# A routed two-layer kernel: a raw weight ring of ten, scaled results inside the next short visit, a relu moved from VectorE to ScalarE

## The chip, the cores and the metric

One core of one Trainium2 chip runs the whole program in one launch. The metric is the time of one execution on the device in microseconds (us). Names used below: TensorE (PE in the rows; PEld is its weight load), VectorE (DVE), ScalarE (ACT), GpSimd (POOL), and SyncE (SP), which issues most of the transfers.

## The reference, cut to what matters

```python
# q, k, v: (8, 8, 576, 64): banded attention (window 128), heads side by side give x: (8, 576, 512)
for b in range(B):
    prev_e = -1
    for s in range(S):
        fresh_e = int(np.argmax(logits[b, s]))
        e = fresh_e if s == 0 or local_gate[b, s] < 0.5 else (prev_e if prev_e >= 0 else fresh_e)
        prev_e = e
        p = softmax(logits[b, s])
        h = np.maximum(x[b, s] @ w1[e], 0.0)      # 512 -> 1024
        out[b, s] = p[e] * (h @ w2[e])            # 1024 -> 512
```

Each of the 4608 tokens goes through one of 8 experts. An expert is two matrix products with a relu between them, and the token's result is scaled with its probability.

## The kernel before, in words

The first third of the span computes attention and the routing. Then follow the **visits**: the plan (PLAN) holds 15 of them, three with the first tokens of experts 0 to 2 (256, 384 and 384 tokens) and twelve ordered by how full an expert is: 512, 272, 384, 232, 384, 232, 384, 200, 416, 264, 168 and 160 tokens. The change and the prediction deal with the last three, called here visit 264, visit 168 and visit 160.

**One visit.** It runs over 8 blocks f of 128 hidden units. For each block TensorE computes the first layer into a PSUM tile `h` (tiles `ah`, `al` of a weight chunk against the tokens' `qx`), then the second layer of the block before it into `y`: `second(f - 1)` stands behind the first layer of block f, and `second(7)` at the end. Every value is held as a coarse part and a remainder (hh and hl, `cut[:, 0]` and `cut[:, 1]`), so each product is three matmuls (lines L1331 to L1333). Between the layers ScalarE and VectorE turn `h` into `hh` = relu(h) and `hl` = relu(h) - hh.

**Visits under 200 tokens** (`both`, visits 168 and 160) compute the first layer in 8 wider matmuls per block (L1403, L1405) into two halves of `h`. ScalarE copies one half to `ha` (L1412), VectorE adds the other (L1413), VectorE makes `hh` (L1421) and `hl` (L1424).

**The partial window.** Tokens beyond a whole number of 128 (16, 8, 40 and 32 tokens in visits 272, 264, 168 and 160, likewise 32 in visit 416) take another way: ScalarE makes `hr` = relu (L1419), and `beside` multiplies it with the raw weight chunk (L1375) in `groups` row groups of one PSUM bank, 4 groups or, in visit 168, 2. At a visit's end `finish` scales the groups: ScalarE scales the first (L1340), VectorE adds the others one after the other (L1343). Whole windows are scaled by ScalarE (L1340) or VectorE (L1338). The scaled tile `y` is stored by an indirect transfer of POOL (L1318).

**Weights.** A weight matrix comes in chunks of 128 x 2 x 512 numbers (512 KB). `Stream.load` issues the transfer of chunk n into `wraw` (6 buffers) as soon as n is under the oldest chunk still needed + 6; a chunk that `beside` will read stays until it is read. `Stream.fill` cuts up to 6 chunks ahead: per chunk two casts by ScalarE (L310) and two subtractions by VectorE (L312) into `cut`. The buffer of a cut chunk comes free when the last matmul that reads it has run.

**Order.** In the visits the order of each engine's instructions is decided when the program is built, by a scheduler that keeps dependencies and places the rest by its own costs; on the chip each engine takes its instructions in that order. What it made of the change is shown below from the built programs.

Of the kernel before, what the change touches and what calls it, by code (L numbers as in the profile page):

```python
# [1 line left out]

# [1 line left out]

# [14 lines left out]
P = 128  # L19
# [15 lines left out]
RAWS = 6  # L35
SPLITS = 6
AHEAD = 4
EARLY = [(2, 5), (3, 6), (3, 6)]

def _plan():  # L40
# [55 lines left out]
def moe_attention(ctx, tc, qT, kT_d, vv, wg, wl, w1, w2, out):  # L96
# [199 lines left out]
            r.gate(t)  # L296
            r.turn(t)

    def load_chunk(e, which, c):
        src = w1 if which == "a" else w2  # L300
        t = wr.tile([P, 2, DM], F32, name="wraw")
# [13 lines left out]
    class Stream:  # L315
# [5 lines left out]
            self.raw, self.cut, self.gone, self.n_raw, self.n_cut, self.first, self.depth = [], {}, set(), 0, 0, 0, 1  # L321

        def load(self, ahead=RAWS):
            while self.n_raw < len(self.order) and self.n_raw < min([self.n_cut, *self.kept]) + ahead:
                e, which, c = self.order[self.n_raw]
                self.raw.append(load_chunk(e() if callable(e) else e, which, c))
                self.n_raw += 1

        def fill(self):
            while self.n_cut < len(self.order) and self.n_cut < self.first + self.depth:  # L330
# [995 lines left out]
    pending = []  # L1326
# [8 lines left out]
    def finish(o, m, g, col, alt, groups=1):  # L1335
# [8 lines left out]
        pending.append((col[:m], y[:m]))  # L1344


    class Fixed:
# [6 lines left out]
        def columns(self):  # L1354
            return 96 * self.rows.tokens + (24 * self.whole + 8 * self.part) * DM

        def run(self, W, tick):
            N = self.rows.tokens
            wins = [slice(P * t, min(P * t + P, N)) for t in range(self.n)]
            ys = [py.tile([P, DM], F32, name="y") for _ in wins]  # L1360
# [4 lines left out]
            both = N < 200  # L1365
            w = P * self.whole if m else N

            def beside(f):
# [12 lines left out]
                raws.clear()  # L1381

            def second(f):
                hh, hl = hs.pop(f)
                vh, vl = W.at("b")
                if m:
                    beside(f)
                for t in range(self.whole):
                    sl = wins[t]
                    three(ys[t][:sl.stop - sl.start], hh[:, sl], hl[:, sl], vh[:, f % 2], vl[:, f % 2], f == 0, f == 7)  # L1390
                    if t == (self.n + 1) // 2 - 1:
                        tick()
                if f % 2:
                    W.done("b")

            for f in range(8):
                ah, al = W.at("a")
                hp = ph_.tile([P, 2 * N if both else N], F32, name="h")
                for kc in range(4):
                    cs = slice(P * kc, P * kc + P)  # L1400
                    if both:
                        passed[0] += 3 * N
                        nc.tensor.matmul(hp.rearrange("p (two n) -> p two n", n=N), ah[:, f % 2, cs], self.rows.x[:, :, kc, :N],  # L1403
                                         start=kc == 0, stop=False, skip_group_check=True)
                        nc.tensor.matmul(hp[:, :N], al[:, f % 2, cs], xh[:, kc], start=False, stop=kc == 3, skip_group_check=True)  # L1405
                    else:
                        three(hp, ah[:, f % 2, cs], al[:, f % 2, cs], xh[:, kc], xl[:, kc], kc == 0, kc == 3)
                    if kc == 1:
                        tick()
                if both:  # L1410
                    ha = mp.tile([P, N], F32, name="ha", bufs=2)
                    now.act.copy(ha, hp[:, N:])  # L1412
                    nc.vector.tensor_tensor(ha, hp[:, :N], ha, ALU.add)  # L1413
                    hp = ha
                hh = mp.tile([P, N], F32R, name="hh", bufs=3)[:, :w]
                hl = mp.tile([P, N], F32R, name="hl", bufs=3)[:, :w]
                if m:
                    rest.append(mp.tile([P, 64], F32, name="hr", bufs=8)[:, :N - w])
                    now.act.activation(rest[-1], hp[:, w:], AF.Relu)  # L1419
                if both:  # L1420
                    nc.vector.tensor_scalar(hh, hp[:, :w], 0.0, None, ALU.max)  # L1421
                else:
                    now.act.activation(hh, hp[:, :w], AF.Relu)  # L1423
                nc.vector.scalar_tensor_tensor(hl, hp[:, :w], 0.0, hh, ALU.max, ALU.subtract)  # L1424
                hs[f] = (hh, hl)
                if f % 2:
# [5 lines left out]
            second(7)  # L1432
            for i, t in enumerate([self.n - 1, *range(self.n - 1)] if m else range(self.n)):
                c = self.rows.t0 + t
                finish(ys[t], wins[t].stop - wins[t].start, self.rows.g[:, t:t + 1], self.rows.idx[2][:, c:c + 1], i % 2 and groups < 4,
                       groups if m and t == self.n - 1 else 1)


    class Flex:
# [25 lines left out]
        def run(self, W, tick):  # L1465
# [49 lines left out]
            second(1, 0)  # L1515
            second(1, 1)
            finish(y, P, self.g, self.scol, 0)

    visits, tile_at = [], TO[0]
    for kind, e, at, nb, n in PLAN:  # L1520
# [93 lines left out]
    for i, v in enumerate(visits):  # L1614
        if isinstance(v, Fixed):
            upto = i + 1
            while upto < len(visits) and isinstance(visits[upto], Flex):
                upto += 1
            v.run(W, lambda: feed.tick(upto))
            feed.finish(upto)  # L1620
        else:
            v.run(W, lambda: feed.tick(upto, False))
# [56 lines left out]
```

## Time and profile before

| what | us |
|---|---|
| time of the runs, median of 3 | 669.78 (669.09 to 672.09) |
| time of the profiled execution | 671.84 |
| its span, first to last instruction | 670.1 |
| TensorE busy | 644.6 |
| VectorE busy | 512.4 |
| ScalarE busy | 412.9 |
| POOL busy | 370.6 |
| mean granted TensorE clock, share of full speed | 0.985 |

The span is what the profile's rows divide; the profiled execution took 1.74 us more than its span. A row of the timeline gives start and duration in us, engine, line, operation, the tiles written and read, the shapes, how many instructions were joined in the row, and in square brackets the engine's idle time before it and what ended it. "Busy" of TensorE is drawn from modelled ends, so two matmul rows may overlap.

### The profile page before, as it was taken

What the parts mean: (1) busy time and instruction counts of PE and PEld (TensorE: products, weight loads), DVE (VectorE), ACT (ScalarE), POOL (GpSimd) and SP (SyncE); (2) the same over time, 40 slices, a digit from 0 to 9 for tenths busy, and PEclk for the clock granted to TensorE, in tenths of its full rate; (3) what the DMA queues carried; (4) which work ended last, traced back from release to release, by engine and by line L of the source; (5) the groups of instructions that cost most, each with busy time, mean ns of one, the idle gap of its engine ahead of it and who ended that gap; (6) DMA issues with size and microseconds to landing.
All of it is one profiled execution on the core that took longest, in us unless ns stands there. A gap on an engine that the chain in (4) does not pass through costs nothing. (4 is left out here: it accounts for less than half of the span.)

```text
span 670.1 us, 17317 instructions
## 1 busy us (share of the span) xinstructions
PE 644.6 (96%) x5913; PEld 515.0 (77%) x5913; DVE 512.4 (76%) x1882; ACT 412.9 (62%) x1148; POOL 370.6 (55%) x567
## 2 busy tenths in 40 slices
PE   6999999999998989999999999999999999999995
PEld 3676766766665877899888889889988988888663
DVE  7899999999998799896454995675676576566883
ACT  4999999999887563344343554553555455455651
POOL 6456466455856776277651847557476466526411
PEclk7999999999998999999999999999999999999998
DMA  9863965853933674465632576666566574447640
GB/s 284 290 212 120 266 188 150 265 168 114 303 110 108 200 237 159 137 209 159 192 92 95 181 258 181 206 207 203 162 216 207 160 237 118 148 134 226 216 158 21
DMA packets 61964, 122.22 MB, mean 182 GB/s; under 512 B 9687, under 2 KB 28759, under 8 KB 61874
## 3 DMA queue, kind: packets, MB, share of 16 engines
q1 hardware_dynamic: 52322, 101.27, 47.9%
q0 software_dynamic: 9120, 19.24, 9.5%
q8 instruction: 47, 0.77, 0.5%
q10 hardware_dynamic: 432, 0.59, 0.3%
q14 instruction: 43, 0.35, 0.2%
HBM read 102.08 MB, written 19.04 MB: 181 GB/s over the span
## 5 line engine op out<-in xcount | busy, mean ns | idle before, releaser
L242 POOL DMA_INDIRECT kr<-xd,xidx x141 | 158.1, 1122 | 57.8 <-issue 41.6
L312 DVE TENSOR_TENSOR cut<-wraw,cut 128x512 fp32r<-128x512 f32 x232 | 151.4, 687 | 31.1 <-ACT cut L310 30.0
L310 ACT CAST cut<-wraw 128x512 fp32r<-128x512 f32 x222 | 127.0, 618 | 42.1 <-PE y L1333 40.2
L1331 PE MATMUL h<-qx,cut 128*128 128x384 f32 (+7 forms) x408 | 130.4, 320 | 1.7 <-ACT qx L253 1.7
L1332 PE MATMUL h<-qx,cut 128*128 128x384 f32 (+7 forms) x408 | 130.2, 319 | 0.1
L1333 PE MATMUL h<-qx,cut 128*128 128x384 f32 (+7 forms) x408 | 130.2, 319 | 0.0
L226 ACT ACTIVATE cut<-scs,mn 128x192 f32<-128x192 f32 (+2 forms) x288 | 121.1, 436 | 14.4 <-DVE mn L226 13.6
L1331 PE MATMUL y<-cut,hh 128*128 128x512 f32 (+2 forms) x288 | 115.4, 401 | 2.7 <-DVE hh L1421 2.7
L226 POOL TENSOR_SCALAR cut<-cut,r 128x192 f32<-128x192 f32 (+2 forms) x205 | 84.7, 429 | 58.6 <-DVE r L226 17.1
L1318 POOL DMA_INDIRECT out<-y,sidx x41 | 43.9, 1072 | 132.2 <-ACT y L1340 69.6
L1333 PE MATMUL y<-cut,hl 128*128 128x512 f32 (+2 forms) x288 | 114.2, 396 | 0.1
L1332 PE MATMUL y<-cut,hh 128*128 128x512 f32 (+2 forms) x288 | 113.6, 394 | 0.0
L1424 DVE SCALAR_TENSOR_TENSOR hl<-h,hh 128x384 fp32r<-128x384 f32 (+4 forms) x104 | 51.2, 495 | 64.2 <-ACT hh L1423 63.9
L1423 ACT ACTIVATE hh<-h 128x384 fp32r<-128x384 f32 (+4 forms) x98 | 43.7, 446 | 84.5 <-PE h L1333 81.2
L226 PE MATMUL sc<-kr,qx 64*64 64x192 f32 (+2 forms) x1152 | 83.0, 332 | 6.3 <-DVE mn L226 6.3
L1331 PEld LDWEIGHTS h<-qx,cut 128*128 128x128 f32 x408 | 77.4, 190 | 7.4 <-ACT qx L253 2.2
L1332 PEld LDWEIGHTS h<-qx,cut 128*128 128x128 f32 x408 | 77.7, 190 | 5.0 <-DVE qx L255 0.4
L1333 PEld LDWEIGHTS h<-qx,cut 128*128 128x128 f32 x408 | 77.7, 190 | 1.3
L226 PE MATMUL xa<-pts,cut 64*64 64x64 f32 (+1 forms) x1280 | 72.1, 254 | 2.5 <-ACT xT L226 2.2
L1331 PEld LDWEIGHTS y<-cut,hh 128*128 128x128 f32 (+2 forms) x288 | 53.5, 186 | 21.1 <-DVE hl L1424 3.3
L226 PEld LDWEIGHTS xa<-pts,cut 64*64 64x64 f32 (+1 forms) x1280 | 48.1, 135 | 23.9 <-issue 8.7
L226 PE MATMUL pt<-ident,cut 128*128 128x128 f32 x384 | 64.1, 289 | 0.7 <-POOL cut L226 0.7
(237 smaller groups left out, 1043.0 us busy)
## 6 DMA issues: line engine op xcount, KB each, us to landing
wraw<-w SPq DMA_DIRECT2D x120, 512.0 KB
kr<-kT SPq DMA_DIRECT2D x31, 288.0 KB
qx<-qT SPq DMA_DIRECT2D x30, 288.0 KB
cut<-v SPq DMA_DIRECT2D x8, 1024.0 KB
xd<-T SPq DMA_DIRECT2D x8, 640.0 KB
xd<-T SPq DMA_DIRECT2D x8, 512.0 KB
kr<-xd,xidx POOLq DMA_INDIRECT x141, 3.7
v<-v SPq DMA_DIRECT2D x16, 128.0 KB
```

Of the source, the lines that this page charges most:

```text
L226: ins = getattr(self.engine, name)(*args, **kw)
L242: queued(nc.gpsimd.indirect_dma_start(out=r, out_offset=None, in_=src[0:n, :], in_offset=bass.IndirectOffsetOnAxis(ap=col, axis=0), bounds ...
L310: scalar.copy(c[:, 0, f], raw[:, f])
L312: vector.tensor_tensor(c[:, 1, f], raw[:, f], c[:, 0, f], ALU.subtract)
L1318: ins = nc.gpsimd.indirect_dma_start(out=out[:, :], out_offset=bass.IndirectOffsetOnAxis(ap=col, axis=0), in_=y, in_offset=None, bounds_ch ...
L1331: nc.tensor.matmul(o, ah, bh, start=start, stop=False)
L1332: nc.tensor.matmul(o, ah, bl, start=False, stop=False)
L1333: nc.tensor.matmul(o, al, bh, start=False, stop=stop)
L1423: now.act.activation(hh, hp[:, :w], AF.Relu)
L1424: nc.vector.scalar_tensor_tensor(hl, hp[:, :w], 0.0, hh, ALU.max, ALU.subtract)
```

## The change

Three edits reach the built program.

1. From chunk 24 on (the first chunk after the three expert visits at the start) raw chunks go through ten places: the six of `wraw`, and four in two tiles `xT` of two chunks each, buffers that attention has left.
2. A visit followed by one under 200 tokens (visits 264 and 168) no longer scales its results at its end: the scalings wait in `late`, and one of them is written into the next visit behind each of its blocks. Banks of the next visit are taken when its second layer begins.
3. The relu `hh` of visits under 200 tokens moves from VectorE (L1421) to ScalarE, and in all visits ScalarE makes `hh` before `hr`. In the last visit the addition of groups stands behind both scalings.

A variable `lag` sets how far the second layer runs behind; its value 1 is what the code before did.

```diff
+    def place(self, n):
+        at = (n - WIDER) % (RAWS + 4) - RAWS
+        if n < WIDER or at < 0:
+            return None
+        if at % 2 == 0:
+            self.both = tp.tile([P, 2, 2, DM], F32, name="xT")
+        return self.both[:, at % 2]
...
+    def finishes(keep=0):
+        while len(late) > max(keep, 0):
+            late.pop(0)()
...
-        for j in range(1, groups):
+        def add(j):
             at = P // groups * j
             nc.vector.scalar_tensor_tensor(y[:m], o[at:at + m], g[:m], y[:m], ALU.mult, ALU.add)
...
+            at = len(late) if back else 0
+            late[at:at] = [partial(add, j) for j in range(1, groups)]
...
+                now.act.activation(hh, hp[:, :w], AF.Relu)
                 if m:
                     rest.append(mp.tile([P, 64], F32, name="hr", bufs=8)[:, :N - w])
                     now.act.activation(rest[-1], hp[:, w:], AF.Relu)
-                if both:
-                    nc.vector.tensor_scalar(hh, hp[:, :w], 0.0, None, ALU.max)
-                else:
-                    now.act.activation(hh, hp[:, :w], AF.Relu)
                 nc.vector.scalar_tensor_tensor(hl, hp[:, :w], 0.0, hh, ALU.max, ALU.subtract)
                 hs[f] = (hh, hl)
+                finishes(len(late) - 1)
...
-                if f > 0:
-                    second(f - 1)
+                if f >= lag:
+                    second(f - lag)
...
-                finish(ys[t], ...)
+                late.append(partial(finish, ys[t], ...))
+            held[0] = self.n
+            if not short:
+                finishes()
+                held[0] = 0
```

TensorE has the same matmuls before and after, in the same order but for a few first-layer matmuls at the start of visits 168 and 160. Lines of the changed kernel are higher by 2 to 41 (L1340 is L1364, L1343 is L1368, L1412 is L1453, L1413 is L1454, L1419 is L1461, L1423 is L1458, L1424 is L1462, L310 is L313, L312 is L315, L249 is L251, L253 is L255, L255 is L257, L1338 is L1362).

**ScalarE, start of visit 168.** Before, from the casts ahead of visit 264's scalings to the second block's copy:

```order
L1340 ACTIVATE y<-y,gs 8x512
L1340 ACTIVATE y<-y,gs 128x512
L310 CAST cut<-wraw 128x512 x2
L1340 ACTIVATE y<-y,gs 128x512
L1412 COPY ha<-h 128x168
L1419 ACTIVATE hr<-ha 128x40
L1412 COPY ha<-h 128x168
```

and of the change:

```order
L1364 ACTIVATE y<-y,gs 128x512
L313 CAST cut<-wraw 128x512 x2
L1364 ACTIVATE y<-y,gs 128x512
L1364 ACTIVATE y<-y,gs 8x512
L1453 COPY ha<-h 128x168
L1458 ACTIVATE hh<-ha 128x128
L1461 ACTIVATE hr<-ha 128x40
L1453 COPY ha<-h 128x168
L313 CAST cut<-xT 128x512 x2
L1458 ACTIVATE hh<-ha 128x128
L1461 ACTIVATE hr<-ha 128x40
L1453 COPY ha<-h 128x168
```

The three scalings of visit 264 still stand ahead of the first copy of visit 168; that of the 8 leftover tokens went from first to last.

**VectorE, the same place.** Before, from the additions of visit 264's groups to the transpose of the next tokens (`xtr`):

```order
L1343 SCALAR_TENSOR_TENSOR y<-y,gs 8x512 x2
L312 TENSOR_TENSOR cut<-wraw,cut 128x512 x2
L1343 SCALAR_TENSOR_TENSOR y<-y,gs 8x512
L1413 TENSOR_TENSOR ha<-h,ha 128x168
L1421 TENSOR_SCALAR hh<-ha 128x128
L1424 SCALAR_TENSOR_TENSOR hl<-ha,hh 128x128
```

and of the change, to the same transpose and on to the third block's `hl`:

```order
L1368 SCALAR_TENSOR_TENSOR y<-y,gs 8x512
L1454 TENSOR_TENSOR ha<-h,ha 128x168
L1368 SCALAR_TENSOR_TENSOR y<-y,gs 8x512
L1462 SCALAR_TENSOR_TENSOR hl<-ha,hh 128x128
L1454 TENSOR_TENSOR ha<-h,ha 128x168
L1368 SCALAR_TENSOR_TENSOR y<-y,gs 8x512
L315 TENSOR_TENSOR cut<-xT,cut 128x512
L1462 SCALAR_TENSOR_TENSOR hl<-ha,hh 128x128
L315 TENSOR_TENSOR cut<-xT,cut 128x512
L251 STREAM_TRANSPOSE xtr<-kr 128x512
L1454 TENSOR_TENSOR ha<-h,ha 128x168
L257 TENSOR_TENSOR qx<-xtr,qx 128x4x128
```

Before, two additions were done ahead of the two subtractions; now all three stand behind them, one ahead of the first block's `ha`, one ahead of its `hl`, one behind the second block's `ha`.

**ScalarE, third and fourth block of visit 168.** Before:

```order
L253 CAST qx<-xtr 128x4x128
L1419 ACTIVATE hr<-ha 128x40
L310 CAST cut<-wraw 128x512 x2
L1412 COPY ha<-h 128x168
L310 CAST cut<-wraw 128x512
L1419 ACTIVATE hr<-ha 128x40
L310 CAST cut<-wraw 128x512
```

and of the change:

```order
L255 CAST qx<-xtr 128x4x128
L1458 ACTIVATE hh<-ha 128x128
L1461 ACTIVATE hr<-ha 128x40
L313 CAST cut<-xT 128x512 x2
L1453 COPY ha<-h 128x168
L313 CAST cut<-xT 128x512 x2
L1458 ACTIVATE hh<-ha 128x128
L1461 ACTIVATE hr<-ha 128x40
```

Behind the cast of the next tokens stand now two instructions of the third block instead of one, and the fourth block's `hr` has four casts and its `hh` ahead of it instead of three casts.

## Rows read from the trace of the kernel before

**Rows 1.** The page: busy time, share of the span, instructions.
```profile
PE 644.6 (96%) x5913; PEld 515.0 (77%) x5913; DVE 512.4 (76%) x1882; ACT 412.9 (62%) x1148; POOL 370.6 (55%) x567
```
**Rows 2.** Windows: length, busy us (x) of PE, PEld, DVE, ACT, POOL, clock, DMA.
```profile
300.00:360.00 60.00, 60.00 (x278) 51.13 (x277) 31.46 (x51) 24.40 (x45) 31.95 (x30) 1.00 0.43 133
...
600.00:620.00 20.00, 20.00 (x129) 17.14 (x127) 12.89 (x25) 11.25 (x31) 13.57 (x13) 1.00 0.67 213
620.00:644.00 24.00, 22.60 (x122) 15.45 (x121) 20.93 (x50) 16.04 (x40) 6.92 (x6) 1.00 0.69 223
644.00:660.00 16.00, 14.68 (x96) 12.21 (x97) 11.22 (x31) 6.92 (x22) 2.30 (x2) 1.00 0.16 55
```
**Rows 3.** Waits of TensorE, 300 to 670: total us, times, longest.
```profile
PE y L1331 <- DVE hh L1421: 2.7, 2, 1.4
```
**Rows 4.** Waits of ScalarE, 280 to 670, the one on a transfer.
```profile
ACT cut L310 <- DMA wraw<-w: 1.5, 1, 1.5
```
**Rows 5.** Timeline, end of visit 264 and start of visit 168.
```profile
621.25 1.50 ACT L1340 ACTIVATE y<-y,gs 8x512 f32<-8x512 f32 x2 [0.94 <-PE y L1375]
622.75 1.14 ACT L310 CAST cut<-wraw 128x512 fp32r<-128x512 f32 x2
623.41 1.29 DVE L312 TENSOR_TENSOR cut<-wraw,cut 128x512 fp32r<-128x512 f32 x2
623.80 0.68 ACT L1340 ACTIVATE y<-y,gs 128x512 f32<-128x512 f32 x1
624.38 0.29 ACT L1412 COPY ha<-h 128x168 f32<-128x168 f32 x1
624.74 0.75 DVE L1343 SCALAR_TENSOR_TENSOR y<-y,gs 8x512 f32<-8x512 f32 x1
625.52 0.33 DVE L1413 TENSOR_TENSOR ha<-h,ha 128x168 f32<-128x168 f32 x1
625.88 0.27 DVE L1421 TENSOR_SCALAR hh<-ha 128x128 fp32r<-128x128 f32 x1
626.21 0.50 PE L1331 MATMUL y<-cut,hh 128*128 128x512 f32 x1 [1.40 <-DVE hh L1421]
```
**Rows 6.** Timeline, third and fourth block of visit 168.
```profile
628.31 0.70 DVE L249 STREAM_TRANSPOSE xtr<-kr 128x512 f32<-128x512 f32 x1
...
630.12 1.14 ACT L310 CAST cut<-wraw 128x512 fp32r<-128x512 f32 x2 [0.32 <-PE y L1333]
...
632.34 0.24 ACT L1419 ACTIVATE hr<-ha 128x40 f32<-128x40 f32 x1 [0.32 <-DVE ha L1413]
...
632.82 1.06 PE L1375 MATMUL y<-wraw,hr 128*40 128x512 f32 x4
```
**Rows 7.** Timeline, last block of visit 168.
```profile
641.15 1.89 PE L1375 MATMUL y<-wraw,hr 128*40 128x512 f32 x4
...
641.70 0.24 ACT L1419 ACTIVATE hr<-ha 128x40 f32<-128x40 f32 x1 [0.32 <-DVE ha L1413]
```
**Rows 8.** Timeline, start of visit 160.
```profile
643.97 1.14 ACT L310 CAST cut<-wraw 128x512 fp32r<-128x512 f32 x2 [0.21 <-PE y L1333]
...
645.95 0.75 DVE L1338 TENSOR_SCALAR y<-y,gs 128x512 f32<-128x512 f32 x1
...
646.62 0.32 DVE L1413 TENSOR_TENSOR ha<-h,ha 128x160 f32<-128x160 f32 x1
...
647.29 0.50 PE L1331 MATMUL y<-cut,hh 128*128 128x512 f32 x1 [1.32 <-DVE hh L1421]
```
**Rows 9.** Timeline, end of visit 160 and the last stores.
```profile
659.83 0.23 ACT L1419 ACTIVATE hr<-ha 128x32 f32<-128x32 f32 x1 [0.39 <-DVE ha L1413]
...
664.50 0.88 POOL L1318 DMA_INDIRECT out<-y,sidx  x1 [0.45 <-DVEq L1629]
```
**Rows 10.** Windows around the one drop of the clock behind attention, columns as in rows 2.
```profile
245.00:248.00 3.00, 1.55 (x7) 0.90 (x5) 3.00 (x10) 2.54 (x5) 1.72 (x2) 1.00 0.88 284
...
250.00:255.00 5.00, 5.00 (x21) 4.91 (x21) 4.43 (x18) 0.71 (x2) 3.98 (x4) 0.66 0.88 311
```

More of the change, by code (lines that the diff above doesn't have):

```diff
@@ L3 @@
 import numpy as np
+from functools import partial
 import concourse.bass as bass
@@ L37 @@
 AHEAD = 4
+WIDER = 24
 EARLY = [(2, 5), (3, 6), (3, 6)]
@@ L297, in at_once, with load_chunk @@
             r.turn(t)
-    def load_chunk(e, which, c):
+    def load_chunk(e, which, c, t=None):
         src = w1 if which == "a" else w2
-        t = wr.tile([P, 2, DM], F32, name="wraw")
+        if t is None:
+            t = wr.tile([P, 2, DM], F32, name="wraw")
         if isinstance(e, int):
@@ L323, in load, with free @@
         def load(self, ahead=RAWS):
-            while self.n_raw < len(self.order) and self.n_raw < min([self.n_cut, *self.kept]) + ahead:
+            while self.n_raw < len(self.order) and self.free(min([self.n_cut, *self.kept]), ahead):
                 e, which, c = self.order[self.n_raw]
-                self.raw.append(load_chunk(e() if callable(e) else e, which, c))
+                self.raw.append(load_chunk(e() if callable(e) else e, which, c, self.place(self.n_raw)))
                 self.n_raw += 1
+        def free(self, used, ahead):
+            n = self.n_raw
+            if n < WIDER:
+                return n < used + ahead
+            at = (n - WIDER) % (RAWS + 4)
+            if n < WIDER + RAWS + 4:
+                return n < used + RAWS if at < RAWS else True
+            return n + (at >= RAWS and at % 2 == RAWS % 2) < used + RAWS + 4
+        def place(self, n):
[5 more added lines that the diff above has]
+            return self.both[:, at % 2]
         def fill(self):
@@ L1333, in three, with finish @@
         nc.tensor.matmul(o, al, bh, start=False, stop=stop)
-    def finish(o, m, g, col, alt, groups=1):
+    def finish(o, m, g, col, alt, groups=1, back=False):
         y = mp.tile([P, DM], F32, name="y", bufs=4)
@@ L1355, in columns, with run @@
             return 96 * self.rows.tokens + (24 * self.whole + 8 * self.part) * DM
-        def run(self, W, tick):
+        def run(self, W, tick, last=False, short=False):
             N = self.rows.tokens
             wins = [slice(P * t, min(P * t + P, N)) for t in range(self.n)]
-            ys = [py.tile([P, DM], F32, name="y") for _ in wins]
+            ys = []
             xh, xl = self.rows.xh[:, :, :N], self.rows.xl[:, :, :N]
@@ L1365, in run, with banks @@
             both = N < 200
+            lag = 1
             w = P * self.whole if m else N
+            def banks():
+                if not ys:
+                    while late and held[0] + self.n > 4:
+                        late.pop(0)()
+                        held[0] -= 1
+                    ys.extend(py.tile([P, DM], F32, name="y") for _ in wins)
             def beside(f):
@@ L1381, in beside, with second @@
                 raws.clear()
-            def second(f):
+            def second(f, rests=True):
                 hh, hl = hs.pop(f)
                 vh, vl = W.at("b")
-                if m:
+                banks()
+                if m and rests:
                     beside(f)
@@ L1428, in run @@
                 tick()
-                if f > 0:
-                    second(f - 1)
+                if f >= lag:
+                    second(f - lag)
                 tick()
-            second(7)
-            for i, t in enumerate([self.n - 1, *range(self.n - 1)] if m else range(self.n)):
-                c = self.rows.t0 + t
-                finish(ys[t], wins[t].stop - wins[t].start, self.rows.g[:, t:t + 1], self.rows.idx[2][:, c:c + 1], i % 2 and groups < 4,
-                       groups if m and t == self.n - 1 else 1)
+            if last and both:
+                W.at("b")
+                beside(7)
+            for f in range(8 - lag, 8):
+                second(f, not last)
+            for i, t in enumerate([self.n - 1, *range(self.n - 1)] if m and not short else range(self.n)):
+                c = self.rows.t0 + t
+                late.append(partial(finish, ys[t], wins[t].stop - wins[t].start, self.rows.g[:, t:t + 1], self.rows.idx[2][:, c:c + 1],
+                                    i % 2 and groups < 4, groups if m and t == self.n - 1 else 1, last))
+            held[0] = self.n
+            if not short:
+                finishes()
+                held[0] = 0
     class Flex:
@@ L1618, in moe_attention @@
                 upto += 1
-            v.run(W, lambda: feed.tick(upto))
+            v.run(W, lambda: feed.tick(upto), i == len(visits) - 1, i + 1 < len(visits) and visits[i + 1].rows.tokens < 200)
             feed.finish(upto)
```

10 lines of the change are left out of this document (8 added, 2 removed).

## The prediction

> **What bounds the kernel now.** I read the page first, for the engines' shares: TensorE is busy 644.6 us of 670.1 [rows 1], and no other engine comes near. Such a share is an average, so the windows came next, and the reader is to see two regimes in them [rows 2]. From 300 to 360 and from 600 to 620 us TensorE has no idle time (60.00 of 60, 20.00 of 20). From 620 to 644 it lacks 1.40 us and from 644 to 660 it lacks 1.32 us, and there VectorE is at 20.93 of 24 us. The waits of TensorE say the same: from 300 to 670 us there are two, 2.7 us together, both for the relu `hh` of VectorE [rows 3]. The timeline shows them, 1.40 and 1.32, as the starts of visits 168 and 160 [rows 5, 8].
>
> A third wait hides in a busy row: in the last block of visit 168 the leftover matmuls take 1.89 us [rows 7] where the same four take 1.06 [rows 6]. Their second half waits for `hr`, which ends at 641.94. So 0.83 us more. What the change could win in these visits is 1.40 + 1.32 + 0.83 = 3.55 us, 0.53% of the time. The waits do not come from missing weights: ScalarE waited for a raw chunk once behind 280 us, 1.5 us [rows 4], while TensorE went on.
>
> At either start the chain is: cut casts, subtractions, leftover scalings, `ha`, `hh`, second layer, and VectorE is the link that ends last. At visit 168 `ha` is copied at 624.38, and its addition starts only at 625.52, because an addition of visit 264's groups stands ahead of it from 624.74 [rows 5].
>
> **Ten raw places.** They remove no work: the same chunks, casts and subtractions. What they can take away is waiting for a raw chunk: 1.5 us of ScalarE, beside a TensorE without idle time [rows 2, 4]. I cost it at 0. SP issues the loads earlier, and what stands behind a load on its queue moves with it; the same cover holds. Bounds: a gain of 1.5 us if that wait were on the path, a loss of 1.5 us if the earlier transfers made one such wait elsewhere.
>
> **`hh` before `hr` in visits 272, 416 and 264.** ScalarE's two relus change places; `hr` comes later by one relu. TensorE has no idle time in these visits, so 0; without that cover it is one short ScalarE instruction, 0.29 us at most (the copy [rows 5]), at each leftover group: two in each visit, 1.7 us at the end of the scale, which needs all six on the path.
>
> **Start of visit 168.** Here the order decides, since each engine takes its instructions as written. ScalarE now scales the first whole window ahead of the casts. The casts start no earlier than the last second-layer matmul, which frees their buffer; I keep 622.75 [rows 5]. A cast pair is followed 1.05 us later by the next instruction (622.75 to 623.80), a scaling 0.58 us later (623.80 to 624.38). So: second window 623.80, the 8 leftover tokens 624.38 to 625.06, `ha` 624.96 instead of 624.38. On VectorE the subtractions end as before at 624.70, and then the first addition waits for the leftover scaling: about 625.1. The addition of `ha` follows 0.78 us later (as 624.74 to 625.52), at 625.88, `hh` at 626.24, the second layer 0.33 us behind that: 626.57 instead of 626.21. **The first wait grows by 0.36 us.** It would shrink only if that addition stood behind `ha`.
>
> What is late next: VectorE still owes two additions, which before were done ahead of the subtractions, beside TensorE's last second-layer matmuls. It saves two relus in exchange. So it reaches the transpose `xtr` later by 0.36 + 2 x 0.75 - 2 x 0.27 = 1.3 us: 629.6 instead of 628.31 [rows 5, 6]. Behind `xtr` (0.70) ScalarE waits with the cast of the next tokens, 630.3; that cast (half a pair, 0.57), `hh` and `hr` of the third block (0.2 us apart) let the next casts start at about 631.25, where before they started with the second layer's end at 630.12. From there to the fourth block's `hr` stand now two cast pairs, a copy and `hh`: 631.25 + 1.05 + 0.2 + 1.05 + 0.2 = 633.75, end 634.0 (634.2 if short instructions don't overlap). The leftover matmuls, which need it, started at 632.82 and now get their second half at 634.0 to 634.2, so **the visit is 1.2 to 1.4 us late there; I take 1.2**, as the rows show ScalarE's instructions overlapping. It contains the 0.36. In the later blocks VectorE has no additions and no relus to do, and catches up; nothing is lost further, nothing won back, since TensorE is then the limit.
>
> **Last block of visit 168.** `hr` stands behind `hh` now, so the wait in [rows 7] grows by one short relu that overlaps: 0.2 us (0 to 0.29).
>
> **Start of visit 160.** ScalarE scales the whole window, VectorE the 40 leftover tokens, where before it was the other way round. The casts set the pace again: 643.97, then on VectorE subtractions, one scaling at 645.95, `ha` at 646.62 [rows 8]. The new scaling of VectorE is as wide and stands in the same place; ScalarE's `ha` comes at 643.97 + 1.05 + 0.58 = 645.6, before VectorE wants it. So the wait of 1.32 us stays: 0. Bounds: 0.75 us less or more, one scaling.
>
> **The end.** The last `hr` (659.83) is later by 0.2 us as well, the rest is the same chain: leftover matmuls, scaling, three additions, the store at 664.50 [rows 9]. 0.2 us.
>
> **The sum.** 0 + 0 + 1.2 + 0.2 + 0 + 0.2 = 1.6 us. The profiled execution, 671.84 us with a span of 670.1, would come to 673.4; the median of the runs shown lies 2.06 below it. **I predict 669.78 + 1.6 = 671.4 us.** The three runs lie 3 us apart, so about 0.5% is what a measurement of this kernel tells from no change.
>
> [...]
>
> **The rivals.**
>
> *VectorE's relief wins (faster).* Sixteen relus of 0.27 us leave VectorE, 4.3 us of its work in visits 168 and 160, and a relu on ScalarE runs beside its additions. If VectorE's load alone makes the waits, all three go: 3.55 us, 666.2 us. For it: 20.93 of 24 us. Against it: the first wait ends on an order, not on a load, and the order now has an addition ahead of the first `ha`. It decides from the point where the leftover scaling ends before 624.4 on ScalarE, which the order excludes. Half of it, 1.8 us, would need the backlog behind the start to vanish as well.
>
> *The ring wins, or nothing changes.* The ring's bound of 1.5 us, or a backlog that is absorbed in the later blocks: 668.3 to 670.5. Against the ring: rows 2 and 4. For absorption: from 644 to 660 VectorE is at 11.22 of 16 us, so it is free late; but the lost time lies earlier, where TensorE can't win it back.
>
> [...]
>
> **Chances.** Forecast (0.6 to 2.6 us slower) 0.60; the ring or nothing 0.18; relief 0.09; clock 0.13. Faster by over 0.5% (under 666.4) needs the whole of the relief: 0.06. Slower by over 0.5% (over 673.1) is half of the clock's chance and the upper tail of the forecast: 0.14. The range 668.0 to 673.6 leaves out the relief and the upper end of the clock.
>
> **What would show it.** In the profile of the changed kernel: TensorE still without idle time from 300 to 620; at the start of visit 168 a wait of about 1.8 us that ends on ScalarE's `hh`; VectorE's additions of 0.75 us around its first `ha`; `xtr` over 6 us behind the first cast pair of that visit (5.56 before); one row of leftover matmuls in the middle of the visit that takes well over 1.06 us; a wait of about 1.3 us at visit 160. I am wrong if the first wait is under 1 us, if TensorE has new waits before 620, or if the clock's windows near the end read under 1.00.

## The result, and the profile after

The changed kernel took 673.03 us (median of 13 runs, 672.16 to 675.85) beside 669.78 us of the kernel before in 13 runs: a ratio of 1.0051, 95% interval 1.0039 to 1.0063. It is slower by 3.3 us, 1.6 us more than predicted: inside the range of 668.0 to 673.6 us, but above the 0.6 to 2.6 us of the forecast itself. The profiled execution took 674.05 us with a span of 672.3. Timed a second time (below) it came to 1.0032, 1.0017 to 1.0047, or 2.3 us between the medians. The traces account for 2.1 us, all in the last two visits; what is known of the rest comes under the experiments.

The page of the changed kernel, as in [rows 1]:

```profile
PE 647.0 (96%) x5913; PEld 514.2 (76%) x5913; DVE 508.7 (76%) x1866; ACT 415.7 (62%) x1164; POOL 370.2 (55%) x567
```

Sixteen instructions went from VectorE to ScalarE, and TensorE does the same work in 2.4 us more of busy time. The windows of the changed kernel, columns as in [rows 2]:

```profile
300.00:360.00 60.00, 60.00 (x278) 51.15 (x277) 31.57 (x51) 24.55 (x45) 32.17 (x31) 1.00 0.46 151
600.00:620.00 20.00, 20.00 (x130) 17.27 (x128) 12.81 (x25) 11.17 (x32) 13.69 (x13) 1.00 0.71 232
620.00:646.00 26.00, 24.57 (x126) 15.98 (x125) 19.38 (x41) 17.20 (x47) 7.34 (x6) 1.00 0.66 226
646.00:662.00 16.00, 14.77 (x92) 11.57 (x93) 9.42 (x23) 8.35 (x30) 1.98 (x2) 1.00 0.06 21
```

TensorE is full up to 620 us as before, and the clock stayed at 1.00 from 600 to 662 us in this execution. VectorE has become freer at the start of the short visits (19.38 of 26 us against 20.93 of 24) and the kernel slower all the same. TensorE's waits from 300 to 670 us are still two, as in [rows 3], but they end on others:

```profile
PE h L1444 <- DVE ha L1454: 1.4, 1, 1.4
PE y L1355 <- ACT hh L1458: 1.2, 1, 1.2
```

And ScalarE's waits on transfers from 280 to 670 us, which were 1.5 us in [rows 4], are 1.7 now, the second of them for one of the new raw places:

```profile
ACT cut L313 <- DMA wraw<-w: 1.0, 1, 1.0
ACT cut L313 <- DMA xT<-w: 0.7, 1, 0.7
```

The stages say where the time went. A stage is here the time from the first first-layer matmul of a visit to that of the next, read from the timelines of TensorE; that of visit 160 runs to the start of its last second-layer matmul, and the tail from there to the end.

| stage, us | before | after | difference |
|---|---|---|---|
| visits 512, 272, 384, ... 264, together (10 stages) | 300.76 | 300.74 | within 0.02 each |
| visit 168 | 21.22 | 22.60 | +1.38 |
| visit 160 | 17.89 | 18.60 | +0.71 |
| tail | 8.46 | 8.47 | +0.01 |

So the loss is 2.1 us, and the two spans differ by 2.2; what differs ahead of visit 512 nearly cancels (the first visit starts 1.72 us later, and the second, of 384 tokens, is 1.57 us shorter). The granted clock differs in just these places: here it read 0.60 and 0.72 from 205 to 210 and 210 to 215 us, and 1.00 from 250 to 255; before it read 0.66, 1.00 and 0.66. By an estimate from these windows, lost clock of 0.06 and 0.28 of 5 us more is 1.7 us, and 0.34 of 5 us less is 1.7 again, which is the size of both.

**Visit 168.** The timeline of the changed kernel at its start, which answers to [rows 5]; the visit's first matmul starts at 622.68 here and at 622.55 before:

```profile
622.68 0.32 PE L1444 MATMUL h<-qx,cut 128*128 128x336 f32 x1
...
623.93 1.24 ACT L1364 ACTIVATE y<-y,gs 128x512 f32<-128x512 f32 x2
625.08 0.27 ACT L1453 COPY ha<-h 128x168 f32<-128x168 f32 x1
625.21 0.74 DVE L1368 SCALAR_TENSOR_TENSOR y<-y,gs 8x512 f32<-8x512 f32 x1 [0.38 <-ACT y L1364]
625.98 0.33 DVE L1454 TENSOR_TENSOR ha<-h,ha 128x168 f32<-128x168 f32 x1
626.35 0.74 DVE L1368 SCALAR_TENSOR_TENSOR y<-y,gs 8x512 f32<-8x512 f32 x1
626.35 0.31 ACT L1458 ACTIVATE hh<-ha 128x128 fp32r<-128x128 f32 x1 [0.99 <-DVE ha L1454]
626.37 0.42 PE L1444 MATMUL h<-qx,cut 128*128 128x336 f32 x1 [1.43 <-DVE ha L1454]
626.71 0.50 PE L1355 MATMUL y<-cut,hh 128*128 128x512 f32 x1
627.69 0.75 DVE L1368 SCALAR_TENSOR_TENSOR y<-y,gs 8x512 f32<-8x512 f32 x1
629.77 0.69 DVE L251 STREAM_TRANSPOSE xtr<-kr 128x512 f32<-128x512 f32 x1
```

The three 8-row additions of visit 264 stand around the first `ha`, one ahead of it as before, two behind. From the visit's first matmul to its second layer there pass 4.03 us; before it was 3.66, counted from this row:

```profile
622.55 0.32 PE L1403 MATMUL h<-qx,cut 128*128 128x336 f32 x1
```

TensorE's wait is shown as 1.43 only because a pair of first-layer matmuls of the third block slipped in ahead of the second layer. `xtr` comes 7.09 us into the visit, 5.76 before. The fourth block carries it on, as in [rows 6]:

```profile
631.36 1.13 ACT L313 CAST cut<-xT 128x512 fp32r<-128x512 f32 x2
632.58 1.14 ACT L313 CAST cut<-xT 128x512 fp32r<-128x512 f32 x2
633.55 1.61 PE L1415 MATMUL y<-wraw,hr 128*40 128x512 f32 x4
633.62 0.31 ACT L1458 ACTIVATE hh<-ha 128x128 fp32r<-128x128 f32 x1
633.83 0.23 ACT L1461 ACTIVATE hr<-ha 128x40 f32<-128x40 f32 x1
```

Two cast pairs stand ahead of `hh` and `hr`, and the leftover matmuls take 1.61 us instead of 1.06, since their second half waits for the `hr` that ends at 634.06. Counted from the visit's first matmul, TensorE begins them 0.60 us later than before, and goes on behind them 1.15 us later. The first row is of the changed kernel, the second of the kernel before:

```profile
635.09 0.50 PE L1355 MATMUL y<-cut,hh 128*128 128x512 f32 x1
```

```profile
633.81 0.50 PE L1331 MATMUL y<-cut,hh 128*128 128x512 f32 x1
```

In the last block they take 2.11 against 1.89 [rows 7]:

```profile
642.44 2.11 PE L1415 MATMUL y<-xT,hr 128*40 128x512 f32 x4
```

**Visit 160.** Its start is as good as before: 3.42 us from the first matmul to the second layer, 3.52 before. The loss is in the third block. Of the changed kernel:

```profile
651.12 0.33 DVE L1454 TENSOR_TENSOR ha<-h,ha 128x160 f32<-128x160 f32 x1
651.65 0.62 ACT L313 CAST cut<-wraw 128x512 fp32r<-128x512 f32 x1 [0.56 <-PE y L1357]
652.17 0.31 ACT L1458 ACTIVATE hh<-ha 128x128 fp32r<-128x128 f32 x1
652.53 0.50 PE L1355 MATMUL y<-cut,hh 128*128 128x512 f32 x1
652.91 0.29 DVE L1462 SCALAR_TENSOR_TENSOR hl<-ha,hh 128x128 fp32r<-128x128 f32 x1
653.25 0.50 PE L1357 MATMUL y<-cut,hl 128*128 128x512 f32 x1
```

and the same block of the kernel before:

```profile
649.67 0.33 DVE L1413 TENSOR_TENSOR ha<-h,ha 128x160 f32<-128x160 f32 x1 [0.20 <-ACT ha L1412]
650.03 0.23 DVE L1421 TENSOR_SCALAR hh<-ha 128x128 fp32r<-128x128 f32 x1
650.03 0.62 ACT L310 CAST cut<-wraw 128x512 fp32r<-128x512 f32 x1 [0.40 <-PE y L1333]
650.84 0.42 PE L1331 MATMUL y<-cut,hh 128*128 128x512 f32 x1
651.33 0.39 PE L1333 MATMUL y<-cut,hl 128*128 128x512 f32 x1
```

Before, VectorE ran `hh` right behind its own addition. Now `ha` is ready at 651.45, but on ScalarE a cast stands ahead of `hh`, and this cast waits until TensorE's previous second-layer matmul has freed its buffer; `hh` starts at 652.17. `hl` then stands behind a subtraction on VectorE (652.30 to 652.99), and the third matmul waits for it: 2.13 us behind the start of `ha`, where it was 1.66. From the visit's first second-layer matmul to its first leftover matmuls there pass 5.97 us, before 5.36. No row of the waits names this: the gaps lie inside groups of matmuls that read as busy. At the visit's end the leftover matmuls take 1.65 us instead of 1.45, behind an `hr` that now follows `hh`. So the 0.71 us are 0.10 won at the start, 0.61 lost up to the first leftover matmuls and 0.20 at the end.

### The profile page after: what moved, and what is told of

It is laid out like the page before. It is cut to its first block, busy times and chain, and to the rows that moved or that the text cites. A ratio compares the mean times of both kernels' runs of the same rounds, so it can differ in the third digit from the quotient of the medians.

```text
span 672.3 us, 17347 instructions
## 1 busy us (share of the span) xinstructions
PE 647.0 (96%) x5913; PEld 514.2 (76%) x5913; DVE 508.7 (76%) x1866; ACT 415.7 (62%) x1164; POOL 370.2 (55%) x567
## 5 line engine op out<-in xcount | busy, mean ns | idle before, releaser
L315 DVE TENSOR_TENSOR cut<-wraw,cut 128x512 fp32r<-128x512 f32 x160 | 104.5, 687 | 25.2 <-ACT cut L313 24.7
L1338 POOL DMA_INDIRECT out<-y,sidx x41 | 44.7, 1091 | 135.5 <-ACT y L1364 69.6
L1458 ACT ACTIVATE hh<-h 128x384 fp32r<-128x384 f32 (+4 forms) x98 | 43.8, 447 | 104.4 <-PE h L1357 101.1
L313 ACT CAST cut<-wraw 128x512 fp32r<-128x512 f32 x150 | 85.6, 618 | 32.2 <-PE y L1357 31.1
L1462 DVE SCALAR_TENSOR_TENSOR hl<-h,hh 128x384 fp32r<-128x384 f32 (+4 forms) x104 | 51.2, 494 | 61.5 <-ACT hh L1458 50.2
L1357 PEld LDWEIGHTS y<-cut,hl 128*128 128x128 f32 (+2 forms) x288 | 53.3, 185 | 15.9 <-DVE hl L1462 3.7
```

Of the source, the lines that this page charges most:

```text
L313: scalar.copy(c[:, 0, f], raw[:, f])
L315: vector.tensor_tensor(c[:, 1, f], raw[:, f], c[:, 0, f], ALU.subtract)
L1338: ins = nc.gpsimd.indirect_dma_start(out=out[:, :], out_offset=bass.IndirectOffsetOnAxis(ap=col, axis=0), in_=y, in_offset=None, bounds_ch ...
```

## The experiments

Three groups of kernels ran on three chips. On the first and the third the kernel before itself took 733.39 and 759.78 us. The traces of the kernels that ran there show idle time that the profile puts down to "issue", and a lower clock, ahead of visit 512 and in some of the visits up to 264: in ring6 the "issue" rows of TensorE's waits from 220 to 560 us add up to 28.7 us and the granted clock from 220 to 480 us read 0.91, visit 512 begins at 365.79 us instead of 321.94, and the ten stages together take 318.30 us instead of 300.74. On the first of them all four kernels read slower than the kernel before by 0.65 to 1.51%, with the ring and without it, which is more than the last two visits hold; ringonly, expected at 1.000, read 1.0124. No trace of the kernel before from there is on record, so what made these ratios stays open, and the total times of these two groups are not used below. The stages of visits 168 and 160 were as on the chip of the comparison (visit 168 takes 22.59 us in ring6 on the first of these chips, and 22.59 and 22.60 in two traces of the changed kernel on the third). The windows from 220 to 480 us show what else differed. Of the changed kernel in the comparison:

```profile
220.00:480.00 260.00, 257.91 (x1478) 221.90 (x1479) 187.70 (x464) 123.44 (x246) 155.04 (x143) 1.00 0.58 188
```

and of ring6 on the first of the other chips, where the stretch covers fewer visits for that reason:

```profile
220.00:480.00 260.00, 222.07 (x1166) 179.46 (x1165) 153.07 (x404) 94.22 (x189) 116.79 (x113) 0.91 0.43 138
```

All stages:

| kernel | visit 168 | visit 160 | tail | time, ratio to before |
|---|---|---|---|---|
| before | 21.22 | 17.89 | 8.46 | 669.78 |
| after | 22.60 | 18.60 | 8.47 | 673.03, 1.0051 (1.0039 to 1.0063) |
| ring6 (after without the ring) | 22.59 | 18.61 | 8.44 | 740.86 beside 733.39, 1.0110 (1.0047 to 1.0173) |
| ringonly (before with the ring) | 21.22 | 17.88 | 8.44 | 742.51 beside 733.39, 1.0124 (1.0062 to 1.0186) |
| nolate (after, no late scalings) | 21.43 | 18.40 | 8.44 | 744.25 beside 733.39, 1.0151 (1.0078 to 1.0224) |
| reluback (after, relu on VectorE) | 22.30 | 18.02 | 8.45 | 741.03 beside 733.39, 1.0065 (1.0012 to 1.0117) |
| beforeagain | 21.22 | 17.89 | 8.46 | 669.99, 0.9999 (0.9985 to 1.0014) |
| afteragain | 23.43 | 18.59 | 8.46 | 672.31, 1.0032 (1.0017 to 1.0047) |
| lagtwo | 19.80 | 16.96 | 8.56 | 667.59, 0.9967 (0.9956 to 0.9979) |
| lagtwolate | 20.93 | 17.15 | 8.33 | 669.24, 0.9995 (0.9983 to 1.0008) |
| lagthree | 19.61 | 17.49 | 8.57 | 762.24 beside 759.78 |

**One part undone or done alone.** *ring6*: the ring off, all else as changed.

```diff
-WIDER = 24
+WIDER = 1 << 30
```

> The changed kernel with six raw places again; late scalings and the relu on ScalarE stay. Theory (the order of the late scalings and the longer relu chain cost 1.4 us in visit 168 and 0.7 us in visit 160, the ring costs and gives nothing): the order in both visits is as in the changed kernel, so span and time stay within 0.5 us of it, about 1.004 of the kernel before; the first wait of visit 168 ends on ScalarE's hh, near 1.8 us with its two first-layer matmuls. Rival (the ring's earlier transfers cost the part of the slowdown that the two visits do not explain, about 1 us): about 1.002.

*ringonly*: the kernel before with the ring.

```diff
-            while ... self.n_raw < min([self.n_cut, *self.kept]) + ahead:
+            while ... self.free(min([self.n_cut, *self.kept]), ahead):
...
-                self.raw.append(load_chunk(...))
+                self.raw.append(load_chunk(..., self.place(self.n_raw)))
```

> The kernel before with ten raw places alone. Theory: 1.000, within 0.3 us, waits of 1.40 and 1.32 us where they were. Rival (the ring costs 1 us): 1.0015. Rival (the ring helps, up to the 1.5 us that ScalarE waited for a chunk): 0.998.

*nolate*: results are scaled at the end of each visit again.

```diff
-            v.run(W, ..., i + 1 < len(visits) and visits[i + 1].rows.tokens < 200)
+            v.run(W, ..., False)
```

> The changed kernel with the scalings at the end of every visit; ring and relu on ScalarE stay. Theory (the slowdown of visit 168 is an order: additions around its first ha): two additions stand ahead of the subtractions again, visit 168 loses its 1.4 us but for 0.2 at its last block, visit 160 keeps the longer relu chain: 0.3 to 0.9 us above the kernel before, 1.0005 to 1.0015. Rival (VectorE's load makes the waits, so its relief wins where the additions are out of the way): 1 us or more under the kernel before, 0.998. Rival (the relu on ScalarE is the cost): stays at 1.003 or more.

*reluback*: the relus in their old order, that of the short visits on VectorE again.

```diff
-                now.act.activation(hh, hp[:, :w], AF.Relu)
                 if m:
...
+                if both:
+                    nc.vector.tensor_scalar(hh, hp[:, :w], 0.0, None, ALU.max)
+                else:
+                    now.act.activation(hh, hp[:, :w], AF.Relu)
```

> The changed kernel with hh of the short visits on VectorE again and hr ahead of hh; ring and late scalings stay. Theory (order of the scalings): the additions still stand around the first ha, and VectorE has the relus as well, so visit 168 is 1.2 to 2 us late, visit 160 not late or up to 0.4: 1.002 to 1.0035. Rival (the relu on ScalarE is the cost of the change): 1.000 to 1.001.

What follows: the ring moves neither stage (by 0.01 us at most, taken off or put in alone). The late scalings, edit 2, cost 1.17 us in visit 168 and 0.20 in visit 160 (after less nolate). The relus, edit 3, cost 0.21 and 0.52 us (nolate less ringonly). These two differences add up to the whole by the way they are taken; a check is to undo the edits the other way round, with reluback: the relus then cost 0.30 and 0.58 us (after less reluback), the late scalings 1.08 and 0.14 (reluback less ringonly). So the split is good to about 0.1 us. For visit 168 the 1.08 us are a little less than reluback's expectation of 1.2 to 2. In nolate the 0.21 us of visit 168 all lie in its last block, whose leftover matmuls take 2.11 us as in the changed kernel.

The third block of visit 160 shows the relu's part. With late scalings gone, but `hh` on ScalarE (nolate), `hh` still stands behind the cast, 0.89 us behind the start of `ha`:

```profile
720.02 0.32 DVE L1454 TENSOR_TENSOR ha<-h,ha 128x160 f32<-128x160 f32 x1
720.38 0.62 ACT L313 CAST cut<-wraw 128x512 fp32r<-128x512 f32 x1 [0.40 <-PE y L1357]
720.91 0.30 ACT L1458 ACTIVATE hh<-ha 128x128 fp32r<-128x128 f32 x1
```

With `hh` on VectorE (reluback) it follows at once, 0.36 us behind, and the stage gets back 0.58 of its 0.71 us. From the first second-layer matmul to the first leftover matmuls there pass 5.01 us instead of 5.97; but the second layer begins 4.00 us into the visit instead of 3.42. The last leftover matmuls take 1.45 us again instead of 1.65. The rows of reluback:

```profile
729.16 0.32 DVE L1454 TENSOR_TENSOR ha<-h,ha 128x160 f32<-128x160 f32 x1
729.52 0.23 DVE L1462 TENSOR_SCALAR hh<-ha 128x128 fp32r<-128x128 f32 x1
```

**The same kernels again.** *beforeagain* is the kernel before without an edit, *afteragain* the changed kernel, with the two next ones on a chip where the kernel before took 669.99 us.

> The kernel before, unchanged, timed against itself, to learn what no change at all reads as. Both theories expect a ratio of 1.000 within 0.003, a stage of 21.2 us for visit 168 and of 17.9 us for visit 160 (to its last second-layer matmul), and a tail of 8.4 to 8.5 us. If the ratio or the share of half clock in its runs differs from that by as much as the 1 us that the two traces leave open, that 1 us is the clock's scatter; if it stays within 0.001, the open 1 us belongs to the change.

> The changed kernel a second time. Theory A (the whole loss is the two short visits: 1.4 us in visit 168, 0.7 in visit 160, and the rest of the 3.25 us between the medians is the clock's scatter): a ratio of 1.002 to 1.004, stages of 22.6 and 18.6 us, and no difference in any other stage of visits. Rival B (the change also costs about 1 us elsewhere, by the earlier weight loads or the clock): 1.005 again, with a granted clock below that of the kernel before in most of its runs.

No change reads as 0.9999, so an interval of 0.0015 either way is what this measurement leaves open. By the expectation a ratio so near to 1 would give the open 1 us of the first measurement to the change; but the changed kernel itself, timed again, lost 2.1 us by its ratio (1.1 to 3.1 by the interval) and 2.3 us between the medians, near the sum of the stages in the first trace. The intervals of its two measurements overlap. Its second trace held a surprise: visit 168 took 23.43 us. The windows of afteragain:

```profile
620.00:625.00 5.00, 3.57 (x23) 2.95 (x22) 3.57 (x7) 4.00 (x11) 2.33 (x3) 1.00 0.92 279
625.00:630.00 5.00, 5.00 (x19) 2.94 (x19) 4.08 (x9) 2.51 (x8) 4.02 (x4) 0.66 1.02 393
```

and of its timeline the first two rows of leftover matmuls of the visit:

```profile
626.60 1.94 PE L1415 MATMUL y<-wraw,hr 128*40 128x512 f32 x4
...
632.23 1.17 PE L1415 MATMUL y<-wraw,hr 128*40 128x512 f32 x4
```

Behind the wait at the start of the visit the granted clock fell to 0.66 of full speed over 5 us (in the trace of the kernel before, a 5 us window of 0.66, from 250 to 255, read 0.50 from 251 to 253 and 1.00 from 254 on); the first leftover matmuls, 1.06 us in the first trace, took 1.94, and the stage is 0.83 us longer than there. A part of the lost time is covered: the fourth block's leftover matmuls, which waited for `hr`, take 1.17 us instead of 1.61. From 205 to 215 us, where it had fallen in the first traces of both kernels, the clock stayed at 1.00.

*afterlook1* and *afterlook2*: the changed kernel, two more traces.

> One more trace of the changed kernel, for the clock alone. In the two traces so far the granted clock read 1.00 through visit 168 in one (stage of 22.60 us) and 0.66 from 625 to 630 us in the other (23.43 us). If the clock falls there in many executions, one of two further traces shows it again, with a stage of over 23.2 us; if it was rare, both show 22.5 to 22.7 us.

> The second of the two: as the first, 22.6 us for visit 168 with the clock at 1.00 there, or over 23.2 us with a window under 1.00 between 620 and 632 us.

Both, on the third chip, show 22.59 and 22.60 us with the clock at 1.00 in that visit. So the drop is there in one of four traces of the changed kernel, and in neither of the two of the kernel before. With it an execution of the changed kernel is 2.9 us behind, without it 2.1: that holds the 2.3 us between the medians of the second measurement and most of the first one's 3.3. Where a timed execution lost clock, no run shows, but the mean granted clock of each is on record. Of the 13 of the first measurement seven read 0.986 to 0.990 and took 672.16 to 673.03 us, six read 0.982 to 0.984 and took 674.05 to 675.85; of the nine of the second, seven read 0.986 to 0.990 (671.22 to 673.06 us) and two 0.983 and 0.984 (673.78 and 673.97). So a part of what the first measurement shows above the second is that more of its executions had a low clock.

**The second layer further behind.** *lagtwo* is the kernel before, with the second layer two blocks behind in visits 168 and 160, and a bank of the second layer for the third block.

```diff
+            spare = py.tile([P, DM], F32, name="y") if N < 200 else None
             ys = [py.tile([P, DM], F32, name="y") for _ in wins]
...
+            lag = 2 if both else 1
...
-                hp = ph_.tile([P, 2 * N if both else N], F32, name="h")
+                hp = spare[:, :2 * N] if both and f == 2 else ph_.tile(...)
...
-                if f > 0:
-                    second(f - 1)
+                if f >= lag:
+                    second(f - lag)
                 tick()
-            second(7)
+            for f in range(8 - lag, 8):
+                second(f)
```

> The kernel before, with the second layer two blocks behind the first in visits 168 and 160 alone, and the third block's first-layer result in one of the four banks of the second layer, so that it needn't wait for the first block's addition. Theory A (what costs time at these starts is the chain copy, addition, relu, which ends 1.3 to 1.4 us after TensorE has run out of first-layer work): a third block of 2.1 us covers the chain, both waits go, the wait of the last block too, up to 3.5 us: the stage of visit 168 takes 19.0 to 19.9 us instead of 21.2, that of visit 160 16.6 to 17.3 instead of 17.9, the ratio is 0.995 to 0.997. Rival B (VectorE is the limit of these stages, 20.93 of 24 us, whatever the order): the waits come back at a later block, the two stages together win under 1 us, 0.999 or more.

The two stages win 1.42 and 0.93 us, the ratio is 0.9967 (0.9956 to 0.9979): by 0.3% faster than the kernel before, with every instruction of it. The expectation held for both stages and the ratio; but the third block is about 1.06 us of TensorE's work, not the 2.1 written there, and so the chain is covered but for a rest. The rest, and the leftover matmuls of the last block, in the trace of lagtwo:

```profile
625.04 0.47 PE L1331 MATMUL y<-cut,hh 128*128 128x512 f32 x1 [0.42 <-ACT ha L1414]
...
639.30 1.06 PE L1377 MATMUL y<-wraw,hr 128*40 128x512 f32 x4
...
645.12 0.50 PE L1331 MATMUL y<-cut,hh 128*128 128x512 f32 x1 [0.79 <-DVE hh L1423]
```

The waits of 1.40 and 1.32 us are down to 0.42 and 0.79, and the 1.89 us of the last block's leftover matmuls are the plain 1.06. VectorE's load is the same (23.60 us from 620 to 646, in lagtwo as in beforeagain), so what went of these waits was not made by its load.

*lagtwolate* is the changed kernel with the same distance and bank.

```diff
-            lag = 1
+            lag = 2 if both else 1
+            spare = py.tile([P, DM], F32, name="y") if both else None
...
-                hp = ph_.tile([P, 2 * N if both else N], F32, name="h")
+                hp = spare[:, :2 * N] if both and f == 2 else ph_.tile(...)
```

> The changed kernel with the same two blocks of distance in visits 168 and 160 and the same spare bank; it keeps the raw ring, the late scalings and the relu on ScalarE. Here ScalarE copies the first block ahead of the casts and VectorE adds it behind one addition only. Theory A (late scalings and the longer relu chain cost time only because the second layer waits for the chain): the loss of 2.1 us in the two stages vanishes with the waits, the stages come to 19.0 to 20.0 and 16.6 to 17.5 us, as in the kernel before with two blocks of distance, within 0.5 us, ratio 0.995 to 0.998. Rival B (the additions and ScalarE's extra relus delay whatever follows, the next tokens' transpose and the casts): the stages stay at least 1 us behind those of the kernel before with two blocks of distance, and the middle of visit 168 keeps a row of leftover matmuls of over 1.5 us.

Between the two theories: visit 160 is 0.19 us behind that of lagtwo (0.71 at a distance of one), but visit 168 still 1.13 us, and the ratio is 0.9995. The row of over 1.5 us that the rival expected in the middle of visit 168 is not there: the leftover matmuls of the middle blocks take 1.06. Its rows:

```profile
625.07 0.50 PE L1355 MATMUL y<-cut,hh 128*128 128x512 f32 x1 [0.70 <-ACT hh L1459]
...
639.91 1.32 PE L1416 MATMUL y<-xT,hr 128*40 128x512 f32 x4
```

Of the 1.13 us, 0.28 are there when the second layer begins (4.03 us into the visit, lagtwo 3.75), 0.48 at the first leftover matmuls and 0.74 at the second and 0.86 at the last; there 0.26 more are lost, since they take 1.32 us against 1.06. That the 0.86 us are the late additions' and the 0.26 the relu's is likely by their 1.17 and 0.21 us at a distance of one, but not shown: no run has one of the two edits without the other at a distance of two.

*lagthree* is lagtwo with three blocks.

```diff
-            lag = 2 if both else 1
+            lag = 3 if both else 1
...
-                hh = mp.tile([P, N], F32R, name="hh", bufs=3)[:, :w]
-                hl = mp.tile([P, N], F32R, name="hl", bufs=3)[:, :w]
+                hh = mp.tile([P, N], F32R, name="hh", bufs=4)[:, :w]
+                hl = mp.tile([P, N], F32R, name="hl", bufs=4)[:, :w]
...
```

> The kernel before with the second layer three blocks behind in visits 168 and 160 alone (four buffers of hh and hl instead of three; the third block's first-layer result in a bank of the second layer, as with two blocks). With two blocks of distance TensorE still waited 0.42 us at the start of visit 168 and 0.79 at that of visit 160, since a block of the first layer is only 1.06 us of work. Theory A (the chain at the start is the only thing that is late): a fourth block ahead covers both rests, visit 168 takes 19.2 to 19.5 us and visit 160 16.1 to 16.3, ratio 0.994 to 0.996. Rival B (the fourth block needs the bank that the second block's addition frees, or the casts of the next chunk, and these are as late): the waits move to the first layer and the two stages stay within 0.3 us of those with two blocks, 19.8 and 17.0, ratio 0.996 to 0.998.

Together the stages are 0.34 us worse than with two blocks: visit 168 wins 0.19 and visit 160 loses 0.53. The rival had it, with the first block's addition in the place of the second's: the fourth block at the start of visit 160 waits for the bank that this addition reads.

```profile
739.16 0.32 DVE L1415 TENSOR_TENSOR ha<-h,ha 128x160 f32<-128x160 f32 x1
739.53 0.41 PE L1405 MATMUL h<-qx,cut 128*128 128x320 f32 x1 [0.99 <-DVE ha L1415]
```

By these two traces, on two chips, two blocks are the better distance.

## Why the prediction was right, and where it was short

The forecast was 1.6 us, slower, by the order of instructions in the two short visits. The mechanism was right, and one term of the sum was put too low. Step by step:

- **Ring, 0.** Shown for the last two visits by ring6 and ringonly; in the changed kernel the ten stages before them are equal within 0.02 us with the ring in place. ScalarE's wait for raw chunks did not even go (1.7 us against 1.5), and TensorE did not feel it.
- **`hh` before `hr` in visits 272, 416, 264, 0.** Their stages are equal within 0.02 us.
- **Start of visit 168, +1.2, and its last block, +0.2.** The stage lost 1.38. The links fit too, counted from the visit's first matmul: the second layer 0.37 us later (forecast 0.36), `xtr` 1.33 us later (1.3), TensorE behind the fourth block's leftover matmuls 1.15 us later (1.2), 0.22 us more in the last block. The runs part the two terms as the forecast did: late scalings 1.17 us, relus 0.21.
- **Start of visit 160, 0.** The start itself was right: 3.42 us against 3.52. But the step stopped at the start, and this is the term that was mis-sized: put at 0, it measured 0.5 us, of which 0.1 was won at the start and 0.6 lost up to the first leftover matmuls, in the third block, where `hh` on ScalarE stands behind a cast that waits for TensorE. That 0.5 lies within the bounds of 0.75 us given for the term is luck: they were drawn for one scaling at the start. For visit 168 the same queue had been followed through to the fourth block; for visit 160 it had not.
- **The end, +0.2.** The last leftover matmuls take 1.65 us against 1.45, and from the first leftover matmuls to the last second-layer matmul the visit takes 9.20 us against 9.01.

The sum with the missing term is 2.1 to 2.2 us, as the stages and the second measurement show. Of the rivals, VectorE's relief is refuted: its load fell (19.38 of 26 us against 20.93 of 24) and the waits hardly (2.6 us against 2.7), nolate has the relief without the late additions and is still 0.21 and 0.51 us slower than the kernel before in the two visits, and lagtwo takes over half of the two waits away (2.72 us are 1.21) at the same load. The clock, with a chance of 0.13 and a part in the upper end of the range, was the author's estimate: the drop of [rows 10], 0.66 from 250 to 255 us, is not at these starts, which kept 1.00 [rows 2], and no run shows what decides whether the clock falls behind a wait (beforeagain, with TensorE busy 3.15 of 5 us from 245 to 250 us as in the first trace of the kernel before, read 1.00 from 250 to 255). That it falls behind these waits is half true: it fell in one trace of four, behind the first wait of visit 168, and the stage was 0.83 us longer; a window under 1.00 there was one of the prediction's own signs of being wrong. The first median alone, 673.03, lies nearer to an estimated 672.2 (the forecast's 671.4 and these 0.83 us) than to the forecast; the stages decide, since the first trace lost its 2.1 us with the clock at 1.00 in both visits. What stays open is the rest of the first measurement's 3.3 us, an estimated 0.4 to 1.2 us by how often the clock fell (3.3 less 2.9 and less 2.1); the second measurement needs none. That 673.03 is still in the range is owed to its upper end, which was drawn for a part of the clock's outcome.

Edit 3, with the relu moved off VectorE, cost 0.73 us here (0.88 by the other order of undoing). VectorE was busy 20.93 of 24 us from 620 to 644 us before, and in this case the move did not pay. `hh` takes 0.31 us on ScalarE and 0.23 to 0.28 on VectorE, but most of the cost is where it stands: ahead of `hr` in the last blocks, and behind a cast in the third block of visit 160. There the relu, ready at 651.45, started at 652.17, behind a cast that started at 651.65, when ScalarE had waited 0.56 us for TensorE.

## What to carry to other kernels

When an instruction of a chain goes to a less busy engine, read what stands ahead of it there and what that waits for: here a 0.3 us relu queued behind a cast that waited for the matmuls of the block before. Follow a moved instruction through every block, not only through the start where the wait was seen. And where an engine runs dry behind a chain at a change of stage, more independent work ahead of the consumer (one block more of distance, in a bank that lay idle) won 0.3% here, which shuffling the chain's links did not. A difference between two medians can hold more than the traces do: read the granted clock of each timed execution before giving all of it to the change.

## What the runs showed that was not expected

- The same wait at the start of visit 168 was followed by a drop of the granted clock to 0.66 over 5 us in one execution and by none in three others; the same kernel can differ by 0.8 us in this place.
- The kernel before took 669.78 and 669.99 us on two occasions, but 733.39 and 759.78 us on other chips, with TensorE busy 222.07 of 260 us in a stretch where it is busy 257.91 here, while the last two visits of the changed kernel took the same time to 0.01 us. The cause was not looked for.
- A row of grouped matmuls hides waits: TensorE's list of waits names 2.6 us of the changed kernel, and the 0.6 us that the third block of visit 160 lost is in none of its rows.
